# Batch 1's first stage by twelve SBUF-to-SBUF DMAs, and the order of the work ahead of the first expert block

## The chip, the cores and the metric

One Trainium2 chip, one of its cores. The metric is the device time of one execution in microseconds (us). TensorE (PE; PEld is its weight load), VectorE (DVE), ScalarE (ACT), GpSimd (POOL) and SyncE (SP, which only issues DMAs here) each work through their own instructions in the order of the program and wait for each other by semaphores. DMAs are issued from the queues of SP, ACT and POOL.

## The reference

An FNet mixing layer, then a mixture of experts with one expert for each token:

```python
# x: (8, 2496, 256)
X = np.fft.fft(x, axis=1)
X = np.fft.fft(X, axis=2)
x = X.real.reshape(8 * 2496, 256)          # 19968 tokens

logits = x @ w_gate                         # 8 experts
expert_idx = np.argmax(logits, axis=1)
gate_w = softmax(logits)[token, expert_idx]
# tokens sorted by expert; for each expert e, with F = 1024:
h = np.maximum(x_sorted[lo:hi] @ w1[e], 0.0)
y_sorted[lo:hi] = h @ w2[e]
out = gate_w[:, None] * y                   # back in the tokens' order
```

## The kernel before, in words

**The Fourier part, one batch at a time.** A batch's 2496 positions are split as 104 times 24. Its input comes in three thirds (`load(b, q)`, 896 KB each, into `xq`, three buffers). *Stage one*: VectorE folds the two mirrored halves of a third (an add over all of it, L321, then `fold_d`, L310 to L312; the last third has an extra piece `pm0`), TensorE multiplies by the cosine and sine table (`half1`, two of the twelve residues s at a time; the sums are in the tile `s`), ScalarE copies the sums to `t1`. *Regrouping*: the second stage needs the data by another partition order. For batches 1 to 7, `first(b)` writes `t1` to the DRAM tensor `Td` (L411; for batch 1 from ACT's queue) and `regroup` reads it back in the new order into `t4s` by two DMAs (L423). For batch 0, `first_whole` uses a second copy of the table, `wp`, whose columns are laid out so that each residue goes by one DMA straight from `t1` to `t4s`: twelve DMAs of 110 KB within SBUF (L375). `natural` copies `wp` into the usual layout, `con["w1"]`, for the later batches. `wp` stands in one of the three buffers that later hold the experts' w2. *Stage two* (`second(b)`): a small product turns one column (`turn_last`, tile `pr`), eleven groups (`p2`, ScalarE copies them to `zz`), ten windows (`p3`: TensorE, then ScalarE's copies `zs` and `lg`, then VectorE's rows, L480, and ScalarE's mirrored half, L454). After each five windows `route` takes the expert of each row and its place among the expert's rows: maximum, ranks by TensorE (`rk`), the exponential on ScalarE (L506), positions (L520 to L525). Ten scatters follow, one for each 128 rows (`send`, an indirect DMA to `Xs` from POOL, L238).

**Experts.** Rows are taken from `Xs` in blocks of 512, 256 or 128 rows of one expert; `rounds()` says how many blocks may be worked when a batch has been routed (round 0: two of 256 and four of 128). `plan` works out on VectorE with many small instructions which expert and which rows each block of a round takes (table `tabs`, L558 to L592); `fetch_weights` loads an expert's two matrices (2 x 1024 KB, L616 and L618), `fetch_rows` its rows (`xb`, L606 and L610) once all of the batch's scatters have landed. A block is VectorE's transpose (L654) and ScalarE's part of it, products `ph` into `hT`, products `py`, a scaled copy, an indirect store to `out`. From round 3 on blocks use a seven-product scheme, whose sums of weights stand in `ws` (class `Left`, two buffers).

**The order of the work.** Generators are advanced in an order written by hand, and this fixes each engine's program. First batch 0's stage one, then batch 0's `second`, and between its steps (numbered k) as many steps of batch 1's stage one (`early`) as `PLAN` says for that k. Three steps of `early` stand ahead of `second(0)`. Steps k of 3 to 7 and 11 to 15 are the ten windows, 8 to 10 and 16 to 18 the routing. Then comes the loop over rounds (L1065 on): `experts` yields after each piece of work, and `side` is advanced meanwhile. Ahead of round 0 `side` weaves `close(0)` (batch 0's two plans) with `mixed(1)`: three steps of batch 2's stage one, then `second(1)` with a step of batch 2's stage one at every other step. `experts` waits for the first plan's table (one step of `side` for each try), fetches block 0's weights, sends the scatters that are left, fetches rows, lets twelve more steps of `side` go by, and starts block 0. SP's queue takes its DMAs in this same order and waits at each until its operands are ready; a DMA also waits until an earlier one that used the same semaphore has landed.

Of the kernel before, what the change touches and what calls it, by code (L numbers as in the profile page):

```python
# [188 lines left out]
PLAN = {3: 1, 5: 1, 7: 1, 11: 1, 12: 1, 13: 2, 14: 1, 15: 1, 16: 1}  # L189
# [28 lines left out]
def kernel(ctx: ExitStack, tc, x, w_gate, w1, w2, out):  # L218
# [107 lines left out]
    def half1(b, q, half, pm, pm0, t1):  # L326
        ps = pm_.tile([NP, 2, D], F32, tag="m", name="s1")
        for i in range(2):
            s = 4 * q + 2 * half + i
            if s < NS - 1:  # L330
                mm(ps[:, i], con["w1"][:, s], pm[:, 2 * half + i])
                continue
            for k, lo, hi in ((NS - 1, 0, H + 1), (NS + 1, H + 1, D)):
                mm(ps[:, i, lo:hi], con["w1"][:, k], pm0[:, lo:hi], True, False)
                mm(ps[:, i, lo:hi], con["w1"][:, k + 1], pm[:, 3, lo:hi], False, True)
        act.copy(t1[:, 2 * half:2 * half + 2], ps[:])
# [80 lines left out]

    base = con["cap"]
# [9 lines left out]
    t4s = cp.tile([128, 2 * HALF, D], F32, name="t4s")  # L428
    zz = cp.tile([128, 2, NW * 128], F32, name="zz")
# [118 lines left out]
    def plan(b, size, k, last):  # L548
# [38 lines left out]
        if not last:  # L587

            vec.tensor_scalar(n[:], ex[:], -1.0, float(k), op0=ALU.mult, op1=ALU.add)
            vec.scalar_tensor_tensor(n[:], n[:], 0.0, nb[:], op0=ALU.max, op1=ALU.min)  # L590
            nxt = one("gone", E)
            vec.scalar_tensor_tensor(nxt[:], n[:], float(size), gone[:], op0=ALU.mult, op1=ALU.add)  # L592
            gone = nxt
        yield
        tabs[b, size, last] = tab
# [27 lines left out]
    class Left:  # L623


        def __init__(self, w1_sb):
            ws = bp.tile([128, 3, F // 2], F32, tag="ws", name="ws", bufs=2)
# [172 lines left out]
    def experts(todo):  # L800
# [257 lines left out]
    for _ in range(3):  # L1058
        next(early)
    for k, _ in enumerate(second(0)):  # L1060
        for _ in range(PLAN.get(k, 0)):
            next(early, None)
        send()
    work = experts(todo)
    steps = {b: mixed(b) for b in range(1, B)}  # L1065
    for b in range(1, B):
# [4 lines left out]
        if b == 1:  # L1071
            side = woven(chain(close(0), through(0)), chain(early, side))
# [77 lines left out]
```

## Time and profile before

| | us |
|---|---|
| median of 4 runs | 1283.64 |
| lowest, highest | 1280.13, 1285.46 |
| the profiled execution's own time | 1284.42 |
| span of its trace | 1282.6 |
| TensorE busy | 1219.5 (95% of the span) |
| VectorE, ScalarE, GpSimd busy | 760.5, 432.1, 444.9 |
| granted TensorE clock, mean | 0.976 |

Times in the trace count from the span's start. In the lines that follow later, a timeline has the start, the length, the engine ("q" added where it is the engine's queue that issues), the line of the kernel, the operation, what it writes and reads, how many instructions are merged, and in brackets how long the engine was idle before and what ended that. "Remote" and "another core or an unknown queue" mean that the profile doesn't know what ended a wait. L223 is the helper through which all matmuls go, so they are told apart by their tiles: `s` stage one, `pr`, `p` and `rk` stage two and routing, `ph` and `py` experts. The chain of work that ended last, followed back from the end, is 89% TensorE; 3% of it are DMAs and 4% VectorE. TensorE's idle stretches of over 0.6 us after 30 us are at 32.25, 40.21, 53.15, 55.50 (12.34 us), 81.91 (4.69 us), 117.45, 122.80 (3.37 us) and 129.07, and eight of at most 2.9 us after 400.

### The profile page before, as it was taken

The page shows a single profiled execution, that of the slowest core. Times are in us where ns is not written, and L with a number is a line of the kernel's source. Part 1 is how long each engine was busy: PE and PEld are TensorE (multiplying, and loading weights), DVE is VectorE, ACT ScalarE, POOL GpSimd, SP SyncE. Part 2 cuts the span into 40 slices and gives each one's busy share as a digit, 9 for nine tenths or more (in the row PEclk, how much of TensorE's full clock was granted, in tenths as well). Part 3 has the DMA queues.
Part 4 walks back from the last instruction along what each step waited for, and adds up shares of the span by engine and source line. Part 5 has one row for each costly group of instructions (what it writes and reads, how often), then busy time and mean ns, then how long its engine had stood idle before and what let it go on. Part 6 is the DMA issues. An engine that isn't in the chain of part 4 may idle for free.

```text
span 1282.6 us, 22389 instructions
## 1 busy us (share of the span) xinstructions
PE 1219.5 (95%) x7317; PEld 1081.1 (84%) x7317; DVE 760.5 (59%) x1820; ACT 432.1 (34%) x1168; POOL 444.9 (35%) x531
## 2 busy tenths in 40 slices
PE   7478999999999999999999999999999999999997
PEld 5457898777787899878998799889999999999996
DVE  4654324343455688557866468676888784445663
ACT  2333332333243433433343333432233232222222
POOL 0337227154126412453215514363265231111112
PEclk8879899999999999999999999999999999999998
DMA  8579599773648334573336424453345327787787
GB/s 240 169 269 352 187 341 310 205 242 123 156 154 247 136 116 165 177 229 117 100 122 203 135 91 128 139 201 108 100 136 159 138 99 264 275 290 282 279 284 277
DMA packets 163062, 248.32 MB, mean 194 GB/s; under 512 B 118542, under 2 KB 130200, under 8 KB 143473
## 3 DMA queue, kind: packets, MB, share of 16 engines
q1 hardware_dynamic: 145644, 201.79, 49.3%
q0 software_dynamic: 16080, 42.85, 9.4%
q10 hardware_dynamic: 1221, 2.24, 0.5%
q8 instruction: 59, 0.97, 0.3%
q14 instruction: 58, 0.48, 0.1%
HBM read 193.45 MB, written 53.45 MB: 192 GB/s over the span
## 4 chain that ended last, share of the span: by engine, by line
PE 89%; DVE 4%; DMA 3%; issue 1%; another core or an unknown queue 1%; ACT 1%; SPq 1%; POOL 0%; POOLq 0%; DVEq 0%; ACTq 0%
PE py L223 24%; PE c L223 13%; PE a L223 12%; PE ph L223 12%; PE e L223 6%; PE b L223 6%; PE d L223 6%; PE p L223 6%; PE s L223 3%; DMA xq<-in_x_dram 2%; DMA xb<-Xs 1%; DVE xq L321 0%; DMA t4s<-Td 0%; PE rk L223 0%
## 5 line engine op out<-in xcount | busy, mean ns | idle before, releaser
L238 POOL DMA_INDIRECT out_dram<-y,ro x163 | 160.7, 986 | 639.4 <-ACT y L750 305.5
L223 PE MATMUL py<-w_sb,hT 128*128 128x256 f32 x1504 | 342.8, 382 | 3.7 <-DVE hT L908 3.7
L223 PEld LDWEIGHTS py<-w_sb,hT 128*128 128x128 f32 x1504 | 282.7, 191 | 42.3 <-DVE hT L908 4.5
L238 POOL DMA_INDIRECT Xs<-rows,pi x160 | 161.5, 1009 | 91.3 <-DVE rows L480 31.8
L223 PE MATMUL ph<-xT,w_sb 128*128 128x128 f32 (+2 forms) x992 | 171.3, 328 | 5.3 <-DVE ro L863 4.7
L223 PEld LDWEIGHTS ph<-xT,w_sb 128*128 128x128 f32 x992 | 136.4, 192 | 29.9 <-issue 17.0
L480 DVE SCALAR_TENSOR_TENSOR rows<-p,zs 128x129 f32<-128x129 f32 x160 | 48.8, 347 | 127.5 <-ACT lg L478 123.8
L223 PE MATMUL a<-xT,w_sb 128*128 128x256 f32 (+1 forms) x512 | 119.6, 361 | 0.1
L908 DVE TENSOR_SCALAR hT<-ph 128x512 f32<-128x512 f32 x43 | 29.7, 691 | 141.0 <-PE ph L223 61.1
L223 PEld LDWEIGHTS a<-xT,w_sb 128*128 128x128 f32 x512 | 90.1, 194 | 11.1 <-DVE xT L654 0.8
L962 ACT ACTIVATE y<-py,xb 128x256 f32<-128x256 f32 x94 | 44.5, 473 | 155.5 <-PE py L223 132.7
L657 ACT ACTIVATE xT<-xT 128x256 f32<-128x256 f32 (+1 forms) x94 | 36.5, 388 | 177.4 <-DVE xT L654 121.6
L706 DVE TENSOR_TENSOR hT<-hT,b 128x512 f32<-128x512 f32 x57 | 39.2, 687 | 87.0 <-ACT hT L703 28.5
L716 ACT ACTIVATE hT<-a 128x512 f32<-128x512 f32 x57 | 34.0, 597 | 143.5 <-PE a L223 102.9
L223 PE MATMUL c<-xT,ws 128*128 128x256 f32 (+1 forms) x256 | 63.7, 377 | 12.4 <-DVE hT L712 11.6
L539 POOL CAST pi<-due 128x1 int32<-128x1 f32 x140 | 41.9, 299 | 84.5 <-ACT due L538 83.9
L223 PE MATMUL a<-w_sb,hT 128*128 128x128 f32 x528 | 66.0, 276 | 0.0
L223 PEld LDWEIGHTS c<-xT,ws 128*128 128x128 f32 x256 | 44.6, 196 | 24.7 <-DVE hT L712 14.5
L223 PEld LDWEIGHTS a<-w_sb,hT 128*128 128x128 f32 x528 | 63.1, 192 | 0.7
L223 PEld LDWEIGHTS p<-table,t4s 120*128 120x128 f32 x352 | 54.4, 205 | 10.6 <-ACT t4s L442 3.7
L223 PE MATMUL p<-table,t4s 120*128 120x120 f32 (+1 forms) x352 | 58.0, 291 | 3.0 <-ACT t4s L442 2.8
L223 PE MATMUL p<-table,zz 128*128 128x145 f32 (+1 forms) x320 | 56.2, 298 | 4.6 <-DVE rows L480 2.1
(163 smaller groups left out, 2077.7 us busy)
## 6 DMA issues: line engine op xcount, KB each, us to landing
w_sb<-in_moe_w_dram SPq DMA_DIRECT2D x132, 1024.0 KB
xq<-in_x_dram SPq DMA_DIRECT2D x23, 896.0 KB
xb<-Xs SPq DMA_DIRECT2D x112, 128.0 KB
Td<-t SPq DMA_DIRECT2D x18, 448.0 KB
t4s<-Td SPq DMA_DIRECT2D x7, 768.0 KB
t4s<-Td SPq DMA_DIRECT2D x7, 640.0 KB
xb<-Xs SPq DMA_DIRECT2D x52, 64.0 KB
xb<-Xs SPq DMA_DIRECT2D x88, 32.0 KB
```

The lines of the kernel that those rows point to most:

```text
L223: nc.tensor.matmul(o, lhsT=lhsT, rhs=rhs, start=start, stop=stop, **kw)
L238: return unordered(pool.indirect_dma_start(out=dst, out_offset=bass.IndirectOffsetOnAxis(ap=idx, axis=0), in_=rows, in_offset=None, bounds ...
L480: vec.scalar_tensor_tensor(rows[:, k + m, 0:NY], p3[:, 0:NY], zs[:, 0:1], zs[:, 1:], op0=ALU.add, op1=op)
L539: pool.tensor_copy(idx, due[:])
L657: act.activation(odd, odd, ACTF.Copy, scale=-1.0)
L706: vec.tensor_tensor(h12, h11, b[:], op=add)
L716: act.activation(h11, a[:], ACTF.Relu)
L908: vec.tensor_scalar(o, ph[:], 0.0, None, op0=ALU.max)
L962: act.activation(y[:, i % 2], py[:], ACTF.Copy, scale=meta[:, i, 1:2])
```

## The change

Batch 1's stage one is given a generator of its own, `first_one`. It uses `wp` (110 columns instead of 112) and sends each residue by one DMA of 110 KB, issued by SP, from `t1` straight into a tile `t4b`; batch 1 no longer touches `Td` and `t4s`, and no DMA of it goes through ACT's queue. `t4b` lies in a new tile `spare` of the same size as the two buffers of `ws`, which it replaces: `Left` takes its two halves in turn. The fold of a third goes in four pieces (two adds over half of it, two `fold_d` over half).

`PLAN` places eleven of its nineteen steps within `second(0)`: the four folds of the first third behind k = 4 to 7, and behind k = 11 to 15 the first third's products, the second third's folds and half of its products. Then come four steps of `close(0)`, which is the whole first plan (its table is now entered ahead of the last `yield`), and then the eight steps left of `first_one` in one piece with a scatter behind each: the last third's folds, the second third's last half product, the last third's products.

In round 0 the first plan's table is there from the start, so no step of `side` goes by while it is waited for. Block 0's weights are fetched first; the load of batch 2's last third is asked for right behind them. Thirteen steps of `side` go by ahead of block 0 instead of twelve; four of these are the second plan's, nine are `mixed(1)`'s: three of batch 2's stage one and the first six of `second(1)`. Before, thirteen steps of `mixed(1)` stood ahead of block 0.

```diff
-PLAN = {3: 1, 5: 1, 7: 1, 11: 1, 12: 1, 13: 2, 14: 1, 15: 1, 16: 1}
+PLAN = {4: 1, 5: 1, 6: 1, 7: 1, 11: 2, 12: 2, 13: 1, 14: 1, 15: 1}
...
     def half1(b, q, half, pm, pm0, t1):
         ps = pm_.tile([NP, 2, D], F32, tag="m", name="s1")
+        n = NR if b == 1 else NP
+        col = (lambda s: wp[:, s]) if b == 1 else (lambda s: con["w1"][:, s])
...
-        act.copy(t1[:, 2 * half:2 * half + 2], ps[:])
+        act.copy(t1[0:n, 2 * half:2 * half + 2], ps[0:n])
...
+    def first_one():
+
+        pm0 = xp.tile([NA, D], F32, tag="pm0", name="pm0")
+
+        def folds(q):
+            xq = ahead[1, q]
+            a, m = xq[:, 0:4], xq[:, 4:8]
+            n = 4
+            if q == NQ - 1:
+                n = 3
+                fold_d(pm0[:], m[:, 3], 1)
+                yield
+            for lo in (0, 2):
+                vec.tensor_tensor(a[:, lo:min(n, lo + 2)], a[:, lo:min(n, lo + 2)], m[:, lo:min(n, lo + 2)], op=ALU.add)
+                yield
+            for lo in (0, 2):
+                fold_d(m[:, lo:lo + 2], a[:, lo:lo + 2], 2)
+                yield
+
+        def products(q):
+            pm = ahead.pop((1, q))[:, 4:8]
+            t1 = xp.tile([NP, 4, D], F32, tag="t1", name="t1")
+            for half in range(2):
+                half1(1, q, half, pm, pm0, t1)
+                for i in range(2):
+                    s = 4 * q + 2 * half + i
+                    nc.sync.dma_start(out=t4b[s:GP:NS, 0:NG], in_=t1[0:NR, 2 * half + i])
+                if half and q < NQ - 1:
+                    load(2, q)
+                yield
+
+        yield from folds(0)
+        yield from woven(products(0), folds(1))
+        yield from woven(products(1), folds(2))
+        yield from products(2)
+        for h in range(2):
+            ahead[1, "t4", h] = t4b[:, h * HALF:(h + 1) * HALF]
...
+    spare = cp.tile([128, 2, 3, F // 2], F32, name="spare")
+    t4b = spare[:].rearrange("p a b f -> p (a b f)").rearrange("p (g d) -> p g d", d=D)
+    turns = [0]
...
-        yield
         tabs[b, size, last] = tab
+        yield
...
-            ws = bp.tile([128, 3, F // 2], F32, tag="ws", name="ws", bufs=2)
+            ws = spare[:, turns[0] % 2]
+            turns[0] += 1
...
                 fetch_some(0, 1)
+                load(2, NQ - 1)
                 while b not in whole:
                     yield 0, True
                 fetch_some(0)
-                for _ in range(12):
+                for _ in range(13):
                     yield 0, False
...
+        if b == 1:
+            yield from first_one()
+            return
         yield from first(b)
         regroup(b, 0)
         regroup(b, 1)
-        if b == 1:
-            load(b + 1, NQ - 1)
...
     early = ahead_of(1)
-    for _ in range(3):
-        next(early)
     for k, _ in enumerate(second(0)):
         for _ in range(PLAN.get(k, 0)):
             next(early, None)
         send()
+    closed = close(0)
+    for _ in range(4):
+        next(closed)
+    for _ in early:
+        send()
...
         if b == 1:
-            side = woven(chain(close(0), through(0)), chain(early, side))
+            side = woven(chain(closed, through(0)), side)
```

More of the change, by code (lines that the diff above doesn't have):

```diff
@@ L327, in half1 @@
         ps = pm_.tile([NP, 2, D], F32, tag="m", name="s1")
+        n = NR if b == 1 else NP
+        col = (lambda s: wp[:, s]) if b == 1 else (lambda s: con["w1"][:, s])
         for i in range(2):
             s = 4 * q + 2 * half + i
+            o = ps[0:n, i]
             if s < NS - 1:
-                mm(ps[:, i], con["w1"][:, s], pm[:, 2 * half + i])
+                mm(o, col(s), pm[:, 2 * half + i])
                 continue
             for k, lo, hi in ((NS - 1, 0, H + 1), (NS + 1, H + 1, D)):
-                mm(ps[:, i, lo:hi], con["w1"][:, k], pm0[:, lo:hi], True, False)
-                mm(ps[:, i, lo:hi], con["w1"][:, k + 1], pm[:, 3, lo:hi], False, True)
-        act.copy(t1[:, 2 * half:2 * half + 2], ps[:])
+                mm(o[:, lo:hi], col(k), pm0[:, lo:hi], True, False)
+                mm(o[:, lo:hi], col(k + 1), pm[:, 3, lo:hi], False, True)
+        act.copy(t1[0:n, 2 * half:2 * half + 2], ps[0:n])
     ahead = {}
@@ L593, in plan @@
             gone = nxt
+        tabs[b, size, last] = tab
         yield
-        tabs[b, size, last] = tab
     def fetch_rows(b, size, tab, i, flat=None):
```

## The prediction

> **What bounds the kernel now.** I read the busy times by stage first. Columns: the stretch, its length, busy time and count of each engine, the granted TensorE clock, DMA share, GB/s.
>
> ```profile
> 26.50:55.50 29.00, 21.54 (x140) 18.23 (x140) 17.96 (x61) 13.45 (x48) 8.13 (x9) 0.93 0.69 207
> 55.50:86.60 31.10, 13.23 (x65) 11.40 (x64) 19.63 (x85) 9.24 (x32) 13.11 (x12) 0.70 0.66 230
> 86.60:140.00 53.40, 48.13 (x234) 40.55 (x234) 19.89 (x72) 16.06 (x62) 29.67 (x44) 0.86 0.85 287
> 140.00:1270.00 1130.00, 1114.16 (x6785) 998.07 (x6784) 687.98 (x1557) 384.55 (x1010) 387.80 (x456) 1.00 0.58 187
> ```
>
> From 140 us on TensorE is busy 1114.16 of 1130 us at full clock. No part of the change lies there, so the end moves by as much as the last experts' work begins earlier or later; the only open time is ahead of 140, above all from 55.5 to 86.6. There I read TensorE's own timeline, ScalarE's, GpSimd's and SyncE's queue:
>
> ```profile
> 55.09 0.42 PE L223 MATMUL rk<-oh,ones 128*128 128x80 bf16 x10
> 67.84 0.54 PE L223 MATMUL pr<-t4s,table 120*120 120x6 f32 x2 [12.34 <-DMA t4s<-Td]
> ...
> 80.80 1.12 PE L223 MATMUL s<-xq,w 104*112 104x256 f32 x4
> 86.60 3.78 PE L223 MATMUL ph<-xT,w_sb 128*128 128x256 f32 x8 [4.69 <-DVE ro L863]
> ```
>
> ```profile
> 52.73 0.17 ACT L478 COPY lg<-p 128x16 f32<-128x16 f32 x1
> 58.69 0.58 ACT L336 COPY t<-s 112x512 f32<-112x512 f32 x1 [5.79 <-remote]
> ...
> 59.97 0.26 ACT L506 ACTIVATE lg<-lg 128x80 f32<-128x80 f32 x1
> ```
>
> ```profile
> 44.93 1.03 POOL L238 DMA_INDIRECT Xs<-rows,pi  x1 [26.56 <-DVE rows L480]
> ...
> 56.77 0.97 POOL L238 DMA_INDIRECT Xs<-rows,pi  x1 [0.30 <-issue]
> 62.58 0.97 POOL L238 DMA_INDIRECT Xs<-rows,pi  x1 [4.84 <-issue]
> ...
> 75.53 0.97 POOL L238 DMA_INDIRECT Xs<-rows,pi  x1 [0.30 <-issue]
> ```
>
> ```profile
> 68.39 0.12 SPq L616 DMA_DIRECT2D w_sb<-in_moe_w_dram  x1
> 68.69 0.35 SPq L618 DMA_DIRECT2D w_sb<-in_moe_w_dram  x1
> 80.84 2.10 SPq L606 DMA_DIRECT2D xb<-Xs  x4
> ```
>
> Two paths meet at 86.60, where the first expert block starts. Path A is batch 0's: windows, routing (its positions end at 61.88), ten scatters from 62.58 to 76.50, their landing until the row fetch at 80.84, the fetch and the transpose: 5.76 us to 86.60. Path B is batch 1's: second stage from 67.84, its rows for ten steps, until the product at 80.80. TensorE stands idle 12.34 and 4.69 us. A decides: B is done at 82, and the idle time ends on the transpose and cast of the fetched rows.
>
> **The change on path A.** *Earlier rows, first half.* Now the vector fold of batch 1 (1.23 + 0.69 + 0.68 + 0.17 us from 31.17) stands ahead of window 0's rows at 33.71, and two half products stand between windows. After, the fold comes in quarters behind windows 1 to 4 and no product is there. Window 0's rows could start at 31.0 (its sums were copied at 30.69 to 31.04), and windows without a product follow each other at 1.15 us (35.36 to 36.51). With the pieces (two adds of 0.69, two folds of about 1.0) that gives the first half's end at 41.9 instead of 44.0: 2.1 us. *Second half.* Four products between its windows become three, the last behind the last window. Steps with a product take 2.1 to 2.4 us (44.03, 46.15, 48.51, 50.76), without one 1.15 and a fold's excess, so 1.3: two of each, 7.0 instead of 8.9 us, 1.9 more. The routing's first step moves from 53.5 to 49.5.
>
> *The unnamed wait.* ScalarE's copy of the last half product waits 5.79 us, although TensorE's sums ended at 53.15 by the timeline, and the exponential behind it moves from 55.2 to 59.97: 4.7 us. What ended it the profile doesn't name. After, a copy still stands ahead of the exponential, but of an ordinary half (1.03 us of matmuls against 1.3). Bounds: all 4.7 gained, or none. The nearest row is this copy itself: batch 1's and 2's twelve executions met it once. I take it as gone. Positions then end at 49.5 + 3.5 (40.49 to 43.96 in the first half) = 53; with the wait at 57.8.
>
> *Scatters.* The first ten then start at 42.9 and need 12.8 us (44.93 to 57.74): 55.7. That is later than 53, so GpSimd decides now: ten more at 13.9 us (62.58 to 76.50) end at 69.8 instead of 76.5, **-6.7 us**. Fetch and transpose keep their 4.3 and 5.8 us: first block at 79.9.
>
> *The queue past which things move.* SyncE issues batch 1's twelve DMAs: 0.76 to 0.92 us each in batch 0's rows, 9.6 us in all. They stand in the queue ahead of the first block's weights, and the load of batch 2's last third (63.61 before) goes behind these weights and ahead of the rows. Weights: last SBUF DMAs issued at about 63.5 (below), weights at 65 instead of 68.39, done in 11 us as before or sooner. The last third's 896 KB stands ahead of the rows at 74: at 329 GB/s (68 to 82) it and the weights' 2 MB take 9 us from 65, to 74. Rows late by 0 to 3 us; I take **+0.5**, since the two meet at 74.
>
> *Path B.* Gone are three writes to Td (ScalarE's queue, 0.31 us each), two reads back (62.51 to 67.70) and their 2.8 MB; added are 1.3 MB within SBUF. Behind routing come now in line: first plan (3.4 us of VectorE's small steps, 61.91 to 67.38 without the folds), the last third's folds (0.55 + 0.95 + 1.36, in more pieces 3.4), last products 1.3, copy 0.6, two issues 1.6: 63.5. These queue behind VectorE's plan; who waits is TensorE's rotation of batch 1, then all of stage two. Landing: batch 0's last issue at 22.40 was not what its reader waited for at 26.55, so at most 4.2 us; far bounds are 0.8 (the issue) and 5.2 (the regrouping, 62.51 to 67.70). With 4.2 stage two starts at 67 instead of 67.84. Only its first three windows now stand ahead of block 0: their rows began 10.6 us after the start (67.84 to 78.42), so 77.6, hidden under A's 79.9.
>
> The DMA rules speak against this part. The Trainium skill, "DMA: Bandwidth & Descriptors", section "Rules for kernel authors", wants small transfers merged, 1 MiB or more per DMA; these have 110 KB. By its fit of about 2.0 us + bytes/436 GB/s each would be an estimated 2.25 us, and stage two would start 2 us sooner than by my row; both leave A deciding. No run shown here merges them.
>
> *Work left behind.* Block 0 starts with less done: two windows with their groups, the ranks and one half product, 2 x 1.05 + 0.5 + 1.0 = 3.6 us of TensorE, must follow. From 92 to 114 TensorE is busy 21.71 of 22 us, so it costs up to 3.6; between 117 and 131 there are 3.37 + 0.96 + 0.64 us of holes that it can fill, so down to 0. I take **+2**.
>
> *Clock.* Through the idle 4.69 us the clock fell: 0.52 from 85 to 92, and eight matmuls took 3.78 instead of 1.89 us, a half product 1.61 instead of 1.03. With 79.9 against 77.6 the hole is 2.3 us: **-2.6**, or 0 if it still falls (the 3.37 us hole at 122.80 was followed by 0.50). "TensorE: Matmul & The Clock Gate", "Part 1: The HAM clock gate", puts the fall at one idle window of about 3.4 us and the recovery at one busy window; here it took some 7 us. By that rule a hole of 2.3 us keeps the clock, the same choice.
>
> The rest hides: the natural copies of the weights for batches 2 and up stay, the products use wp for batch 1 at equal size, and the spare tile that replaces ws has the same two halves and the same readers; it is used again after 400 us, so it costs nothing unless halves were made to wait on each other.
>
> **Sum:** -6.7 + 0.5 + 2 - 2.6 = -6.8 us. The profiled execution took 1284.42 us (span 1282.6), which gives 1277.6; it lies 0.8 above the median of the runs, 1283.64, which gives **1277 us**.
>
> **Rivals.** (1) *The unnamed wait stays.* Positions at 57.8, last scatter at 72.7: -3.8 + 0.5 + 2 - 2.6 = -3.9, 1279.7. For it: the whole trace has four more waits without a name, two of them (117 and 125) where the DMA share is 1.06. (2) *The later hole closes too.* From 117 to 136 VectorE waits 2.72 and 7.38 us in the same unnamed manner, and the clock is at 0.50 for ten; some 10 us. Less DMA traffic and more ready work speak for it, nothing ensures it: up to -16, 1267 with all of it. (3) *Given back at round 1.* Batch 1's routing now starts behind block 0; its twenty scatters ran from 96.80 to 134.17, and the next fetch came at 144.41. If TensorE reaches round 1 before they land, the gain ends there: 1283. Against it: 10 us of slack. (4) *Slower: path B takes over.* Folds, products, copies and DMAs in one line behind the plan. With the unnamed wait, issue ends at 68.1; with 5.2 us of landing and some 2 us in which issues wait for earlier DMAs (batch 0's waited 1.6 us so) stage two starts at 75.5, its third window at 86.1, block 0 at 86.6, and 3.6 us of work is still to do, clock fallen as before: +4, **1288**. It decides as soon as stage two starts later than 71.
>
> **How the numbers follow.** Likeliest case 0.42; (1) 0.15; (2) 0.13; (3) 0.08; (4) 0.22. A measurement of this kernel tells 0.3% (3.9 us) from no change. Faster: nearly all of the likeliest, (2) and some of (1): 0.60. Same: the rest of (1) and most of (3): 0.15. Slower: (4) and a bit: 0.25. The likeliest's own range is 1273 to 1281 (the ends of 0 to 3, 0 to 3.6 and 0 to 2.6 not all at once); with (2) below and (4) above it is 1266 to 1289.
>
> **What would show it.** Right: window 0's rows near 31, first scatter near 43, no break between the tenth and the eleventh, last one near 69, rows fetched near 74, first ph near 80 with the clock kept, no Td for batch 1. Wrong: ph waiting on stage two's windows rather than on the rows; stage two starting after 71; weights or the last third landing after the rows; a new TensorE hole between 80 and 150; gaps at the spare tile after 400.

## The result and the profile after

The changed kernel takes 1286.85 us (median of 49 runs, 1282.39 to 1296.81), the kernel before 1282.59 beside it (75 runs, 1273.12 to 1291.70): 1.0038 of it, with a 95% interval of 1.0026 to 1.0049. It is 4.3 us slower (3.3 to 6.3 by the interval); 1277 was predicted. The profiled execution took 1284.88 us, its span 1283.1. That is only 0.5 us over the span before, less than the runs differ by, because the two traces also differ in spells of half clock long after the change (between 410 and 730 us); what the change itself does is read ahead of 160 us.

First the busy times by stage of the kernel after (columns as in the table of before: stretch, length, PE, PEld, DVE, ACT, POOL, granted clock, DMA share, GB/s).

```profile
26.50:55.50 29.00, 19.99 (x107) 17.59 (x105) 13.24 (x50) 10.85 (x41) 9.84 (x10) 0.74 0.62 170
55.50:86.60 31.10, 16.06 (x71) 13.00 (x71) 18.83 (x85) 7.74 (x23) 11.82 (x10) 0.56 0.63 198
86.60:140.00 53.40, 46.62 (x255) 40.25 (x256) 26.29 (x95) 18.80 (x73) 23.70 (x37) 0.94 0.91 286
140.00:1270.00 1130.00, 1113.76 (x6782) 997.78 (x6781) 688.80 (x1556) 385.84 (x1012) 393.94 (x463) 1.00 0.58 188
```

From 140 us on the busy times hardly differ, as foreseen. Ahead of it the granted clock fell from 0.93 to 0.74 and from 0.70 to 0.56. Now TensorE's, ScalarE's, GpSimd's and SyncE's timelines of the kernel after, and VectorE's one line for the fetched rows:

```profile
67.41 2.90 PE L223 MATMUL s<-xq,wp 104*110 104x256 f32 x6 [5.18 <-issue]
77.38 0.54 PE L223 MATMUL pr<-spare,table 120*120 120x6 f32 x2 [5.37 <-issue]
91.21 3.78 PE L223 MATMUL ph<-xT,w_sb 128*128 128x256 f32 x8 [4.75 <-DVE xT L699]
```

```profile
51.03 0.29 ACT L493 COPY zz<-p 128x160 f32<-128x160 f32 x1 [2.70 <-remote]
53.96 0.27 ACT L519 COPY zs<-p 128x130 f32<-128x130 f32 x1 [2.64 <-PE s L223]
...
56.85 0.27 ACT L519 COPY zs<-p 128x130 f32<-128x130 f32 x1 [2.25 <-remote]
...
59.83 0.27 ACT L550 ACTIVATE lg<-lg 128x80 f32<-128x80 f32 x1 [1.25 <-DVE rows L551]
```

```profile
42.09 1.03 POOL L238 DMA_INDIRECT Xs<-rows,pi  x1 [25.19 <-DVE base L569]
...
53.70 0.97 POOL L238 DMA_INDIRECT Xs<-rows,pi  x1 [0.30 <-issue]
62.45 0.97 POOL L238 DMA_INDIRECT Xs<-rows,pi  x1 [7.77 <-issue]
...
76.00 1.02 POOL L238 DMA_INDIRECT Xs<-rows,pi  x1 [0.30 <-issue]
```

```profile
70.11 4.12 SPq L447 DMA_DIRECT2D spare<-t  x4
76.17 0.38 SPq L660 DMA_DIRECT2D w_sb<-in_moe_w_dram  x1
78.18 0.01 SPq L662 DMA_DIRECT2D w_sb<-in_moe_w_dram  x1
78.22 0.34 SPq L295 DMA_DIRECT2D xq<-in_x_dram  x1
83.05 2.41 SPq L650 DMA_DIRECT2D xb<-Xs  x4
```

```profile
90.44 0.71 DVE L699 STREAM_TRANSPOSE xT<-xb 128x512 f32<-128x512 f32 x1 [2.60 <-DMA xb<-Xs]
```

The first scatter is 2.84 us earlier than before (42.09 for 44.93), but the eleventh comes where it was (62.45 for 62.58): the gain is gone inside the second half of batch 0's windows, where three waits of 2.2 to 2.7 us, two of them without a name, now stand in place of one of 5.79. Behind it the order shows. Weights go out at 76.17 instead of 68.39, since they stand in SyncE's queue behind the last SBUF-to-SBUF DMAs; the last third of batch 2 follows at 78.22; then come the rows. The transpose comes 7.39 us after the fetch of the rows (83.05 to 90.44), where it came 5.0 us after it (80.84 to 85.84). The first ph starts at 91.21 instead of 86.60, 4.6 us later.

These two stretches are not the same wait. In the kernel after, VectorE waits 2.60 us for the rows. In the kernel before it doesn't wait for them at all; it comes to the transpose straight from batch 1's first routing and a fold of batch 2, and its timeline shows no idle time since 80.52:

```profile
80.52 0.61 DVE L480 SCALAR_TENSOR_TENSOR rows<-p,zs 128x129 f32<-128x129 f32 x2 [1.48 <-ACT lg L478]
...
85.77 0.17 DVE L507 TENSOR_SCALAR rows<-table 128x10 f32<-128x10 f32 x1
85.84 0.70 DVE L654 STREAM_TRANSPOSE xT<-xb 128x512 f32<-128x512 f32 x1
```

So the 5.0 us are VectorE's own work for batches 1 and 2, and the rows landed somewhere within them. The change puts that routing behind block 0, and then the landing of the rows shows.

### The profile page after: what moved, and what is told of

Its sections match the earlier page's. It is cut to its first block, busy times and chain, and to the rows that moved or that the text cites. A ratio compares the mean times of both kernels' runs of the same rounds, so it can differ in the third digit from the quotient of the medians.

```text
span 1283.1 us, 22422 instructions
## 1 busy us (share of the span) xinstructions
PE 1221.3 (95%) x7317; PEld 1084.2 (84%) x7317; DVE 762.5 (59%) x1832; ACT 432.5 (34%) x1168; POOL 445.4 (35%) x531
## 4 chain that ended last, share of the span: by engine, by line
PE 71%; issue 18%; POOL 3%; DVE 3%; DMA 2%; ACT 1%; SPq 1%; POOLq 0%; DVEq 0%; ACTq 0%
PE py L223 18%; PE c L223 11%; PE a L223 11%; PE ph L223 6%; PE p L223 6%; PE e L223 5%; PE d L223 5%; PE b L223 5%; PE s L223 3%; POOL out_dram L238 3%; POOL Xs L238 1%; DMA w_sb<-in_moe_w_dram 1%; DMA Xs<-rows,pi 1%; DMA rt<-c_rt 0%; DMA xb<-Xs 0%
## 5 line engine op out<-in xcount | busy, mean ns | idle before, releaser
L223 PE MATMUL c<-xT,spare 128*128 128x256 f32 (+1 forms) x256 | 61.9, 369 | 10.6 <-DVE hT L757 9.3
L223 PEld LDWEIGHTS c<-xT,spare 128*128 128x128 f32 x256 | 43.7, 192 | 22.6 <-DVE hT L757 11.8
L223 PE MATMUL b<-xs,spare 128*128 128x256 f32 (+1 forms) x256 | 59.6, 360 | 0.0
L223 PE MATMUL d<-xT,w_sb 128*128 128x256 f32 (+1 forms) x256 | 59.0, 357 | 0.2 <-ACT y L1008 0.2
```

Source lines behind the costliest of these rows:

```text
L223: nc.tensor.matmul(o, lhsT=lhsT, rhs=rhs, start=start, stop=stop, **kw)
```

## The experiments

Each group of runs ran on one chip, and the five groups on five chips, on which the kernel before took 1256.95, 1256.8, 1282.63, 1265.09 and 1256.35 us. Ratios are to the kernel before on the same chip. The mark used throughout is the start of the **fifth block** (VectorE's cast into `ro` of that block): the work behind it is the same in all kernels (6679 recorded matmuls each time), and from there to the end of the span it is 1106.2 to 1109.2 us in all profiles on the three chips at 1256 to 1257 us. That spread of 3 us is as large as some differences below, so the mark shows where time is lost, and the medians show whether it is. Start times in us, each from one profile:

```
chip  kernel             exp h=1  last scatter  weights  rows fetched  transpose  first ph  fifth block
res.  before               59.97      75.53        68.39      80.84          85.84      86.60      158.35
res.  after                59.83      76.00        76.17      83.05          90.44      91.21      161.57
1     route_only           54.17      69.88        62.36      73.92          80.15      80.91      143.43
1     order_only           53.75      69.91        71.95      77.23          88.30      89.07      155.30
1     all_inside           55.62      70.42        61.60      76.14          80.33      81.10      147.24
1     third_behind_rows    52.71      68.97        69.09      76.72          80.89      81.66      155.53
2     before_again         55.57      71.31        63.81      78.51          83.97      84.72      147.21
2     after_again          51.91      68.44        68.43      76.37          83.55      84.31      150.09
2     inside_16            56.57      71.34        62.51      76.92          82.07      82.83      143.79
2     after_warm           50.03      68.28        65.10      75.56          79.73      80.49      144.40
3     after_16             55.50      72.64        72.75      81.11          92.40      93.16      160.66
3     after_act            60.01      76.16        74.47      84.64          93.66      94.42      162.66
3     after_act_16         58.66      74.81        73.35      83.10         103.11     103.86      171.80
3     route_warm           57.46      73.03        65.50      77.11          83.70      84.45      148.36
4     route_again          58.64      74.20        66.69      77.98          82.25      83.01      147.93
4     inside_16_again      61.51      76.28        67.58      81.73          88.42      89.18      152.70
4     route_15             60.43      76.00        68.47      79.80          88.94      89.70      153.23
5     after_third          54.19      70.35        70.52      77.17          84.62      85.39      151.66
5     tail_first           52.03      68.11        64.73      75.31          79.66      80.43      145.99
5     tail_first_16        54.01      70.04        66.65      79.38          87.59      88.35      149.00
```

### The route alone, and the order alone

`route_only` keeps the order of before and sends batch 1 by the twelve DMAs:

```diff
 # before.py, first(b)
                 half1(b, q - 1, 0, pm, pm0, t1)
+                spread(b, q - 1, 0, t1)      # for b == 1: two DMAs, t1[0:NR] into t4b
...
-        regroup(b, 0)
-        regroup(b, 1)
+        # not for b == 1
```

> The order of before (all of batch 1's first stage inside batch 0's second stage, in the old places), with the new route alone: two SBUF-to-SBUF DMAs per half product in place of Td and the two reads back. Theory 'order' (the last third's folds, products and DMAs, put in one line behind the plan, made stage two of batch 1 start at 77.4 us instead of 67.8; the route itself costs nothing): stage two starts at 65 to 68 us, the first ph at 85 to 87 us, 1280 to 1284 us, not slower than before. Rival 'route' (the twelve DMAs, 4.1 to 6.4 us of SyncE's queue per four, are what is slow): stage two starts after 71 us, 1286 us or more.

Measured: 1251.01 us, **0.9965** (0.9944 to 0.9985). Stage two of batch 1 starts at 62.62 us, the first ph at 80.91. Both came earlier than expected; on that chip everything did. On it the route alone is a gain.

`order_only` is the reverse:

```diff
 # after.py, products(q)
-                for i in range(2):
-                    s = 4 * q + 2 * half + i
-                    nc.sync.dma_start(out=t4b[s:GP:NS, 0:NG], in_=t1[0:NR, 2 * half + i])
+                if half:
+                    act.dma_start(out=Td[1][:, 4 * q * D:4 * (q + 1) * D], in_=...)
...
+            regroup(1, h)
```

> The order of after, with the old route (write to Td, two reads back). Theory 'order': the last product still ends at 72 us, and Td's write and reads (some 5 us by before's rows) replace the last four DMAs, so stage two of batch 1 starts at 77 to 80 us, first ph at 91 to 94 us, 1286 to 1290 us. Rival 'route': stage two starts before 72 us, 1281 to 1284 us.

Measured: 1263.28 us, **1.0046** (1.0026 to 1.0066); stage two at 76.43, the first ph at 89.07, as the order theory had it. What is slow in the change is its order, not its route.

### Where in the order

`all_inside` puts all nineteen pieces between the steps of batch 0's second stage:

```diff
-PLAN = {4: 1, 5: 1, 6: 1, 7: 1, 11: 2, 12: 2, 13: 1, 14: 1, 15: 1}
+PLAN = {4: 1, 5: 2, 6: 2, 7: 2, 11: 2, 12: 3, 13: 3, 14: 2, 15: 1, 16: 1}
```

> After, with all nineteen pieces of batch 1's first stage set between the steps of batch 0's second stage, none left behind the plan. Theory 'order': TensorE has work in its holes again, stage two of batch 1 starts at 66 to 70 us, first ph at 84 to 87 us, 1279 to 1284 us. Rival 'wait' (the wait for TensorE's late semaphore decides, wherever the pieces stand): the positions still end at 61 to 62 us and ph starts at 86 to 87 us, so no better than before, 1282 to 1285 us. Rival 'route': 1286 us or more as after.

Measured: 1258.09 us, 1.0012 (0.9998 to 1.0026). The start of block 0 came as the order theory said, and earlier (first ph 81.10, the route alone 80.91); the time did not follow: the fifth block starts 3.8 us behind that of the route alone, and the medians are 7.1 us apart. TensorE's timeline of this kernel shows it standing still ahead of ph with nothing left to do:

```profile
81.10 1.22 PE L223 MATMUL ph<-xT,w_sb 128*128 128x256 f32 x2 [8.17 <-DVE xT L699]
```

`inside_16` therefore adds three steps ahead of block 0, `range(13)` to `range(16)`:

> After, with all nineteen pieces inside batch 0's second stage, and sixteen steps of the other work ahead of block 0 instead of thirteen. Theory 'work left behind': the run with thirteen steps had an 8.17 us hole of TensorE ahead of the first ph and 3.8 us more up to the fifth block than the run with the new route alone; with sixteen the hole shrinks to 4.5 to 6 us, and the time falls by 3 to 4 us: 0.996 to 0.999 of before. Rival 'load ahead of the rows' (the position of batch 2's last third costs the difference): no change, 1.000 to 1.002.

Measured: 1253.37 us, 0.9980 (0.9965 to 0.9995). The hole is 4.46 us and the fifth block starts at 143.79 for 147.24, 3.45 us earlier. These two profiles are from two chips; on the chip of `inside_16` the kernel before has 147.21. That the idle time was work left behind rests on this one pair.

`third_behind_rows` moves `load(2, NQ - 1)` from right behind block 0's weights to behind its rows:

```diff
                 fetch_some(0, 1)
-                load(2, NQ - 1)
                 while b not in whole:
                     yield 0, True
                 fetch_some(0)
+                load(2, NQ - 1)
```

> After, with the load of batch 2's last third moved from ahead of batch 0's rows to behind them. Theory 'order': the rows still wait for the last scatter and stage two for its DMAs, so ph starts at 90.5 to 91.5 us and the time stays at 1286 to 1288 us. Rival 'load ahead of the rows': rows land up to 2.5 us sooner, ph at 88 to 89 us, 1283 to 1285 us.

Measured: 1264.81 us, **1.0063** (1.0041 to 1.0084), which neither theory had. The rows do come sooner: 4.17 us from fetch to transpose, where after needs 7.2 to 7.5. So the load ahead of the rows does delay them. But VectorE's timeline of this kernel shows the price of putting it behind:

```profile
94.49 0.29 DVE L310 TENSOR_TENSOR pm<-xq 104x127 f32<-104x127 f32 x1 [6.62 <-DMA xq<-in_x_dram]
...
98.24 0.24 DVE L545 TENSOR_TENSOR oh<-table,v 128x80 bf16<-128x80 f32 x1
```

The fold of batch 2's last third is already in VectorE's program, and it waits 6.62 us for the load with batch 1's routing behind it; TensorE then waits 6.78 us for that routing. The load has to be early, but not between the weights and the rows.

### Before and after on one chip, and the clock

`before_again` and `after_again` are the two kernels unchanged.

> The kernel before, profiled on the same chip as the others of this group, so that stage times are compared on one chip. If the wait without a name (ScalarE's copy, 5.79 us at 52.9) belongs to the kernel, the positions of batch 0 end at 61 to 62 us again and stage two of batch 1 starts near 68 us; if it belongs to the chip of the first profiles (the four runs so far don't show it), positions end at 55 to 57 us, stage two starts at 65 to 67 us and the first ph at 80 to 82 us.

> The changed kernel, profiled on the same chip. Theory 'order': whether or not the wait without a name is there, stage two of batch 1 starts 4 to 10 us later than in before, the first ph at 80 to 83 us if the wait is absent (no gain over before there), and the work left behind block 0 makes the time 1.003 to 1.006 of before's. Rival 'wait' (the change is good and only the unnamed wait spoilt it): where it is absent the ratio is 0.996 to 1.000.

Measured: before 1258.13 us in its one run beside a median of 1256.8 of the group; after 1259.21, 1.0023 (1.0007 to 1.0039). ScalarE's wait without a name is in neither. In ScalarE's timeline of `before_again` the copy of the last half product waits 1.09 us for TensorE, and the exponential comes at 55.57:

```profile
54.30 0.58 ACT L336 COPY t<-s 112x512 f32<-112x512 f32 x1 [1.09 <-PE s L223]
55.57 0.26 ACT L506 ACTIVATE lg<-lg 128x80 f32<-128x80 f32 x1
```

So that wait goes with the chip and not with the kernel, and the change is slower without it too. This pair gives the account of the change; beside it the pair of the result:

```
difference, after - before (us)              one chip, no unnamed wait    result
last scatter starts                                   -2.87               +0.47
from there to the fetch of the rows                   +0.73               +1.74
from the fetch to the transpose                       +1.72               +2.39
first ph                                              -0.41               +4.61
from the first ph to the fifth block                  +3.29               -1.39
fifth block                                           +2.88               +3.22
ratio                                                 1.0023              1.0038
```

In the pair on one chip, too, the transpose of before follows VectorE's own work (83.89, then 83.97) and that of after waits for the rows (3.73 us). The two profiled spans are only 0.3 us apart (1256.4 and 1256.7), yet what is lost by the fifth block isn't won back before the very end: TensorE starts its last product of full size at 1238.57 and 1242.16. Then ScalarE's last copy waits 4.99 us for a store in `before_again` and 2.26 in `after_again`.

`after_warm` adds matmuls into a bank that nobody reads, to keep the clock:

```diff
+        if k in WARMER:                 # {8: 24, 13: 8, 14: 8, 15: 8, 16: 20}
+            filler(WARMER[k])
...
+    filler(36)                          # behind the first plan, and again behind the last piece
...
+                filler(18)              # ahead of block 0's transpose
```

> After, with matmuls into an unread bank added in TensorE's holes (24 at the first routing, 8 behind three windows, 20 at the second routing, 36 and 36 in the tail, 18 ahead of block 0), to keep its clock. Rival 'clock': the granted clock from 52 to 85 us is over 0.85 instead of 0.56, stage two of batch 1 starts 2 to 4 us earlier than in after, and the time falls by 3 to 6 us against after. Theory 'order': VectorE's plan and folds and SyncE's DMAs set the tail, so stage two starts at most 1.5 us earlier and the time stays within 2 us of after's.

Measured: 1258.43 us, 1.0012 (0.9997 to 1.0027), against after's 1.0023 (1.0007 to 1.0039): no difference that the runs can tell. Its one profile says more: granted clock 0.89 from 55.5 to 86.6, stage two at 67.55 for 69.65, and the fifth block 5.7 us earlier, span 1251.0. The clock is worth something in that execution; that it is worth so much in the median is not shown.

### On a chip with the wait

Three edits of after, and the route with fillers, on a chip at 1282.63 us. `after_16`: `range(13)` to `range(16)`, nothing else. `after_act`: the last four SBUF-to-SBUF DMAs on ScalarE's queue. `after_act_16`: both. `route_warm`: the route alone, with `filler(10)` at the first routing, `filler(64)` ahead of batch 1's stage two and `filler(18)` ahead of block 0.

```diff
-                    nc.sync.dma_start(out=t4b[s:GP:NS, 0:NG], ...)
+                    (act if q == NQ - 1 else nc.sync).dma_start(out=t4b[s:GP:NS, 0:NG], ...)
```

> After, with sixteen steps of the other work ahead of block 0 instead of thirteen, nothing else. Theory 'work left behind' (the change's loss is what block 0 leaves behind; TensorE stood idle 5.88 us ahead of the first ph with no step left to do): the idle time ahead of ph falls by 2 to 3.5 us, the first ph stays at 83 to 86 us, the fifth block starts 2.5 to 3.5 us earlier than in after, and the time is 0.998 to 1.001 of before. Rival 'late stage two' (batch 1's stage two starts too late by 3 us, so that more of it ahead of block 0 only delays ph): ph at 86 to 89 us, the fifth block where it was, 1.002 to 1.004.

Measured: 1288.52 us, 1.0047 (1.0019 to 1.0075). The fifth block came only 0.9 us earlier than in after's profile of the result, and the time not at all: VectorE reaches the transpose 11.29 us after the fetch, straight from a fold (92.32, then 92.40), so its own steps stood ahead and not the rows.

> After, with the last third's four SBUF-to-SBUF DMAs issued by ScalarE instead of SyncE, so that the first block's weights don't stand behind them. Theory 'queue' (weights and last third, issued 6 us later than with the new route alone, fill the DMA engines while the scatters and then the rows land): weights are issued at 62 to 65 us instead of 68.4, the rows are fetched at 73 to 75.5 us instead of 76.4, ph at 80 to 82 us instead of 84.3, and the time falls by 1 to 3 us against after, 0.999 to 1.002 of before. If the queue doesn't matter: ph at 83.5 to 85 us, 1.002 to 1.004.

Measured: 1291.05 us, **1.0070** (1.0040 to 1.0100), against both readings. It is higher than after's 1.0038 (1.0026 to 1.0049) in the result, but the intervals overlap, and after was not run in this group. ScalarE's timeline shows what was late (its idle time ahead of the first copy of batch 1's stage two):

```profile
72.57 1.60 ACTq L447 DMA_DIRECT2D spare<-t  x2
84.14 0.17 ACT L486 COPY spare<-pr 120x6 f32<-120x6 f32 x1 [11.60 <-PE pr L223]
```

The last two DMAs are issued by 74.2 us, and stage two begins at 83.6: 9.4 us of landing, where the same DMAs on SyncE's queue took 3.2 in after (74.2 to 77.4) and 3.1 in `after_16` on this chip (70.9 to 73.9). VectorE then goes from the third window's rows (93.14) straight to the transpose (93.66): here block 0 waits for stage two, and not for its rows. The weights and the last third went out on SyncE at 74.5 to 76.2 meanwhile, and the DMA share from 75 to 90 us is 1.00 to 1.06. The Trainium skill, "DMA: Bandwidth & Descriptors", section "Issuing engines are not separate DMA queues", says that transfers from different issuing engines share the same 16 engines and interleave; this row agrees: a second queue let 2.9 MB share the engines with 440 KB that were waited for. The profile puts the end of TensorE's wait (11.85 us) down to a DMA of the weights; but of 480 packets of ScalarE's queue 163 moved between 78 and 80 us and the last 7 after 82.

> After with both edits: the last third's four DMAs on ScalarE's queue and sixteen steps ahead of block 0. If the two losses are separate, they add: fifth block 4 to 6 us earlier than in after, 0.996 to 0.999 of before. If one hides the other: as the better of the two.

Measured: 1298.01 us, **1.0113** (1.0062 to 1.0164): the first ph at 103.86. The last DMAs, issued by 73.1, are followed by stage two at 85.93, 12.8 us later. More work ahead of block 0 makes a late stage two dearer.

> The new route alone in the old order, with matmuls into an unread bank added in TensorE's holes (10 at the first routing, 64 ahead of batch 1's stage two, 18 ahead of block 0). If the clock is worth something there: granted clock over 0.85 from 55 to 85 us instead of 0.5 to 0.7, stage two ends sooner and the first eight ph take 1.8 us instead of 3.6, fifth block 1.5 to 3.5 us earlier than with the route alone, 0.993 to 0.996 of before. If the rows decide alone: within 1 us of the route alone, 0.996 to 0.998.

Measured: 1280.41 us, 0.9990 (0.9966 to 1.0014). The fifth block starts at 148.36 in its profile, and that execution's span was 1270.2; the runs lie from 1272.02 to 1285.49. Why the median shows so little of it stays open.

### The route once more, and idle time ahead of block 0

> The new route alone in the old order, once more. Where the kernel before takes some 1257 us it took 0.9965 of it. If this group falls at the 1283 us level instead, where ScalarE's wait without a name is in every profile: the route moves the fifth block by 3 to 6 us there too, 0.995 to 0.999; rival 'level' (at that level the waits that come later give back what the first blocks gain): 0.999 to 1.002.

Measured: 1262.34 us, 0.9983 (0.9959 to 1.0007), on a chip at 1265.09 where the unnamed wait is there (5.42 us). Not proven faster there, and not slower.

> All nineteen pieces inside batch 0's second stage and sixteen steps ahead of block 0, once more. At the 1257 us level 0.997 to 0.999 again. At the 1283 us level, theory 'order': 0.996 to 1.000, since neither stage two nor the last third of batch 2 comes late; rival 'level': 1.001 to 1.004, as the changed kernel itself.

Measured: 1269.48 us, 1.0043 (1.0022 to 1.0064), against 0.9980 on the other chip. Its second half of routing ended late (exponential at 61.5, the route alone 58.64), and the first ph is 6.2 us behind. The repaired order is not repaired everywhere.

`route_15` is the route alone with `range(15)` for `range(12)`:

> The new route alone in the old order, with fifteen steps of the other work ahead of block 0 instead of twelve. TensorE stood idle 4.68 us ahead of the first ph with the route alone; three more steps are some 3.5 us of its work. Theory 'work left behind': ph within 1 us of the route alone's, the fifth block 1.5 to 3.5 us earlier, 0.994 to 0.997 of before, the fastest of the three. If that idle time isn't free (the steps' VectorE and ScalarE work stands ahead of the transpose and the cast that ph waits for): ph 1 to 4 us later, no gain over the route alone.

Measured: 1267.98 us, 1.0027 (1.0008 to 1.0046), slower than `route_again` beside it. The first ph came at 89.70 for 83.01, of which 1.8 us are a stage two of batch 1 that began later by as much (64.30 for 62.49). The rest is in VectorE's timeline of `route_15`:

```profile
82.14 0.24 DVE L516 TENSOR_TENSOR oh<-table,v 128x80 bf16<-128x80 f32 x1
82.30 0.68 DVE L310 TENSOR_TENSOR xq<-xq 104x508 f32<-104x508 f32 x1
...
88.42 0.61 DVE L495 SCALAR_TENSOR_TENSOR rows<-p,zs 128x129 f32<-128x129 f32 x2 [1.36 <-ACT lg L493]
88.94 0.70 DVE L670 STREAM_TRANSPOSE xT<-xb 128x512 f32<-128x512 f32 x1
```

Batch 1's whole first routing, a fold and two windows' rows stand ahead of the transpose, with 2.3 us of gaps in 6.8. In `route_again`, as in the kernel before, only the first part of that routing does (82.17, then the transpose at 82.25). TensorE's idle time ahead of ph is not free, because the steps that would fill it bring VectorE work with them.

### The plan behind the last third

`tail_first` only exchanges two pieces of the change:

```diff
     closed = close(0)
-    for _ in range(4):
-        next(closed)
     for _ in early:
         send()
+    for _ in range(4):
+        next(closed)
```

> The changed kernel once more, profiled and timed beside the next two. Theory 'order': 1.002 to 1.005 of before whatever the level; its rows reach the transpose 7 us or more after their fetch (7.2 and 7.4 us so far, before's 5.0 and 5.5).

> After, with the last third's pieces put ahead of the first plan's four steps instead of behind them. Theory 'order': VectorE's plan (3.4 us) no longer stands ahead of the folds, so stage two of batch 1 starts 2.5 to 4 us earlier than in after; weights and the last third of batch 2, which stand behind the same DMAs on SyncE, go out up to 3 us earlier, the rows reach the transpose 5 to 6.5 us after their fetch, and the time falls by 2 to 4 us against after: 0.998 to 1.001 of before. Rival 'nothing is set by stage two': first windows' rows wait for batch 0's scatters anyway, within 1.5 us of after.

Measured: after 1260.52 us, 1.0040 (1.0027 to 1.0053); `tail_first` 1258.39, 1.0015 (0.9998 to 1.0031). By the medians 2.1 us of the loss are undone, by the ratios 3; the intervals overlap a little. SyncE's and VectorE's timelines, first of `after_third`:

```profile
64.46 4.12 SPq L447 DMA_DIRECT2D spare<-t  x4
70.52 0.38 SPq L660 DMA_DIRECT2D w_sb<-in_moe_w_dram  x1
71.11 0.35 SPq L662 DMA_DIRECT2D w_sb<-in_moe_w_dram  x1
71.56 0.37 SPq L295 DMA_DIRECT2D xq<-in_x_dram  x1
77.17 2.40 SPq L650 DMA_DIRECT2D xb<-Xs  x4
```

```profile
84.62 0.71 DVE L699 STREAM_TRANSPOSE xT<-xb 128x512 f32<-128x512 f32 x1 [2.66 <-DMA xb<-Xs]
```

then of `tail_first`:

```profile
58.98 4.12 SPq L447 DMA_DIRECT2D spare<-t  x4
64.73 0.38 SPq L660 DMA_DIRECT2D w_sb<-in_moe_w_dram  x1
65.32 0.35 SPq L662 DMA_DIRECT2D w_sb<-in_moe_w_dram  x1
65.78 0.36 SPq L295 DMA_DIRECT2D xq<-in_x_dram  x1
75.31 2.40 SPq L650 DMA_DIRECT2D xb<-Xs  x4
```

```profile
79.66 0.71 DVE L699 STREAM_TRANSPOSE xT<-xb 128x512 f32<-128x512 f32 x1 [0.41 <-DMA xb<-Xs]
```

DMAs, weights and last third all go out 5.5 to 5.8 us earlier, stage two starts at 68.5 for 71.8, and the transpose, which waits for the rows in both, comes 4.35 us after the fetch instead of 7.45. The load still stands ahead of the rows, but the engines are freer by then: the DMA share is 0.34 from 78 to 80 us here, and 1.05 from 85 to 90 in after.

> The same with sixteen steps ahead of block 0. Theory 'work left behind' (3.45 us at the 1257 us level, between thirteen and sixteen steps with all pieces inside): another 2 to 3.5 us, 0.996 to 0.999 of before. Rival 'the rows' (at the 1283 us level sixteen steps moved the transpose to 11.4 us behind the fetch and the time did not fall): as tail_first or up to 2 us slower.

Measured: 1257.96 us, 1.0008 (0.9993 to 1.0023): no different from `tail_first`. Its first ph is at 88.35 instead of 80.43, and its fifth block 3 us later in the profile: the start of batch 1's routing and a fold now lie ahead of the transpose, as in `route_15`, and its rows were fetched 4 us later. Sixteen steps gained in one pair (`all_inside` to `inside_16`, on two chips) and in no other.

No version is shown to beat the route alone, the best in both of its groups: 0.9965 and 0.9983.

## Why the prediction was wrong, point by point

**Earlier rows, first half: right.** 2.1 us were claimed for the first scatter; 2.84 and, on one chip, 2.8 (44.73 to 41.92) were measured.

**"A decides": misread in the kernel before.** The prediction let path B end with TensorE's product at 82 and put the idle 4.69 us down to the fetched rows. VectorE's half of path B, with a fold of batch 2 in it, goes on until 85.84 without a gap (the lines above), so B ended that wait. The 5.8 us kept for "fetch and transpose" were the price of this work and not of the rows. The change does bring path A to the front, because it leaves that routing behind block 0.

**The unnamed wait: the step that made the size wrong.** The prediction took 4.7 us as gone, because the copy that waited was moved. The wait goes with the chip: ScalarE shows waits without a name between 46 and 63 us in none of eleven profiles on the three chips at 1256 to 1257 us, the kernel before among them, and in eight of nine on the others, after among them. Why is open. Where it is absent, before has not got it either, so nothing is gained (last scatter -2.87, not -6.7); where it is present, after has three of them. Rival 1 saw the first of this, but put the positions at 57.8; they ended at 61.7, since three copies waited instead of one.

**"Fetch and transpose keep their 4.3 and 5.8 us", and +0.5 for the queue: the step that failed in kind.** On one chip without the wait the last scatter starts 2.87 us earlier and the first ph only 0.41. The prediction had weights at 65 and their traffic done by 74. They went out at 76.17 (68.43 and 70.52 on the other chips), and with the last third they were still on the DMA engines when scatters and rows had to land. +0.5 measured +2.45 on one chip (0.73 + 1.72), +4.1 in the result. `tail_first` and `third_behind_rows` show it: with the bytes moved away, the rows are there 4.35 and 4.17 us after the fetch, against 7.18 to 7.45 in the change. So the late bytes cost the rows some 3 us, more than the table's 1.72, since the 5.46 us of `before_again` are not the rows' landing.

**Why the weights were late: the line behind the plan was mis-sized.** It was summed as plan 3.4, folds 3.4, products 1.3, copy 0.6, issues 1.6. In the result plan and folds took 6.3 (61.8 to 68.1), near enough. The products took from 67.41 to 72.02, 4.6 us for 1.3: they are two half products and not one, at a granted clock of 0.50 behind a hole of 5.18 us. SyncE's last four DMAs took 4.12 us of its queue for 1.6, as two were counted. Landing took 3.2, within the 4.2 allowed. Stage two then starts at 77.38 (69.65 and 71.77 elsewhere) for 67. In the result most of that is the line's late start, at 61.8 instead of 53, which is the unnamed wait again; on the chip of `after_again` it started at 53.9, and the 2.65 us are the line's own.

**Work left behind: mis-sized.** +2 was taken from 0 to 3.6. One chip shows +3.29. In the result it was -1.39: the later hole of 3.37 us at 122.80, rival 2's place, is gone there, and gives some of it back.

**Clock kept: wrong.** Eight ph took 3.78 us as before, in the result and on the one chip. There the holes were 4.75 and 5.88 us and not 2.3, but even a hole near the forecast does not keep it. The two windows tables that follow (stretch, length, busy times, clock, DMA, GB/s) are of `tail_first`, with a hole of 2.55 us ahead of ph at 80.43, and of `after_warm`, with 1.24:

```profile
78.00:80.00 2.00, 0.00 (x0) 0.00 (x0) 0.95 (x3) 0.61 (x3) 0.00 (x0) 1.00 0.34 56
80.00:82.00 2.00, 1.57 (x6) 1.24 (x7) 0.42 (x2) 0.42 (x1) 0.00 (x0) 0.84 0.64 119
82.00:84.00 2.00, 2.00 (x9) 1.72 (x8) 0.00 (x0) 0.60 (x1) 0.00 (x0) 0.50 0.56 79
```

```profile
78.00:80.00 2.00, 1.25 (x12) 0.88 (x9) 0.88 (x3) 0.03 (x1) 0.00 (x0) 1.00 0.39 68
80.00:82.00 2.00, 1.51 (x7) 1.26 (x8) 0.49 (x2) 0.42 (x1) 0.00 (x0) 1.00 0.52 104
82.00:84.00 2.00, 2.00 (x16) 1.90 (x15) 0.00 (x0) 1.17 (x5) 0.00 (x0) 1.00 0.44 61
```

After 2.55 us of nothing the grant falls, and falls when the matmuls have already begun again. (The hole of 2.73 us in `third_behind_rows` was followed by 0.50 too, and its eight ph took 3.60 us.) The Trainium skill, "TensorE: Matmul & The Clock Gate", "Part 1: The HAM clock gate", puts the fall at an idle window of about 3.4 us; these rows differ, and the measurement decides.

**The terms together.** On the one chip the gain at the last scatter is 3.8 us short of the forecast (2.87 for 6.7), the queue cost 1.95 more than allowed, the work left behind 1.29 more, and the clock gave 2.6 less: 9.7 us, from -6.8 forecast to +2.88 at the fifth block.

**Rival 4: the right side, for half of the reason.** It gave 1288 with stage two later than 71, and both came about in the result; on one chip the change was slower with stage two at 69.65. But it had ph wait for stage two's windows. TensorE waited for the transpose (4.75 us, xT), and this for the fetched rows. Rival 4's own wait is in `after_act`. The late line reached block 0 through SyncE's queue: DMAs first, weights behind them, their bytes ahead of the rows.

**Right besides:** no gaps at the spare tile, and the route costs nothing; on one chip it gains.

Still open: what holds ScalarE's copies on some chips (each group had one chip at one time, so the two aren't told apart); why the order with all pieces inside gives 0.9980 on one chip and 1.0043 on another; and why fillers move a profile by 5.7 us and the median by less than the runs can tell.

## What to carry to other kernels

When work is moved behind a stage, follow the queue that its DMAs are issued on: what stands behind them is late by the whole line, and its bytes then meet the next thing that has to land. Compare two orders at a point where both have done the same work (here the fifth block), not at the first thing that starts earlier. A wait without a name in one profile is no gain to book: look whether another chip has it.

## What the runs showed of the hardware

- The same kernel took 1256 to 1283 us on different chips. Waits of ScalarE without a name, the longest of each profile 2.7 to 5.8 us, were in the profiles of some chips and of others not.
- DMAs moved to ScalarE's queue landed later, not sooner: after 9.4 and 12.8 us for 3.1, on one chip. They no longer stood ahead of the 2.9 MB on SyncE's queue, and shared the engines with them.
- The clock fell after a hole of 2.55 us, an estimated 0.9 us into the next matmuls (they began at 80.43; the row from 80 to 82 has 0.84 between one of 1.00 and one of 0.50), and a hole of 1.24 us kept it.
